# Two regroupings and two weight sums moved later, and the first batch's last score tiles in two bank pairs, in a fused attention and gated feed-forward kernel

## The chip, the core and the metric

The kernel runs on one core of a Trainium2 chip. The metric is device microseconds for one execution. Inputs and output are float32 in DRAM, and the products run in bfloat16.

## The reference

```
q, k, v: (8, 12, 448, 64)         w_gate, w_val: (768, 1536)      w_out: (1536, 768)
scores = (q @ k^T) / sqrt(64)
attn   = relu(scores)^2 / 448
o      = attn @ v                                  # per batch and head
x      = o.transpose(0, 2, 1, 3).reshape(3584, 768)
gate   = relu(x @ w_gate);  val = x @ w_val
out    = (gate * val) @ w_out
```

## The kernel before

There are eight batches of 448 tokens and twelve heads. For each batch the kernel makes attention scores, squares their positive part, multiplies with the values into x (768 features of 448 tokens, features on partitions), makes the gated hidden layer hT (1536 x 448) in twelve units, and for every two batches the output product.

TensorE (PE) works on 64x64 quarters: one call of `mm4` issues four matmuls of 64x448 that run at the same time in the four quarters of the array. The text calls four such matmuls a **pass**. The pieces are:

- A **score tile** (`tile_of`) is one pass: 64 keys of four heads against 448 queries, into a pair of PSUM banks. There are 21 for a batch. `relu2` then lets ScalarE (ACT) take the positive part of the pair into `r_sb` (line 234, four buffers), and VectorE (DVE) squares it into `attn` (line 235).
- **Values** (`value_passes`): seven passes over the seven score tiles of four heads, into one bank pair. In the first batch the pair is always banks 6 and 7, called `both`. The result is copied out of PSUM into x: in the first batch by one instruction (lines 660 and 674), later half by ACT (line 268) and half by DVE (line 269). `exchange` (line 263) then copies each half of the partitions into the other half of a second tile, as two DVE instructions.
- A **unit** (`gv_unit`) is twelve passes that accumulate gate in one bank and val in the other bank of a pair. At its end ACT takes relu of gate (line 327) and DVE multiplies it with val into hT (line 328). Two bank pairs, 6-7 and 4-5, take turns (`acc`), so a unit cannot begin in its pair before line 328 of the unit before the last has read it. Score tiles and values of batches from 1 on take turns in banks 0-1 and 2-3 (`sc_later`).

The order on every engine is written out by hand: `pin` keeps the instructions of an engine in program order. In `spread`, the passes of the units of batch b-1 are walked through one by one, and events of batch b (score tiles, values, regroupings, loads) are put in front of the pass (unit, number) that they are listed with. `last` is the last unit of the walk, and `step` adds passes to such a place.

- **Regrouping** (`regroup`, line 180): k and q of a batch are loaded token by token, and before their transposition DVE copies each into `kr` or `qr`, in two halves of 128x1536. `transpose_grouped` then issues DMA transposes from the SP queue. `turned(b, units, place_of_k, place_of_q)` puts the first half of each at its place and the second five passes later.
- **Weight sums** (`weight_sums`, line 352): four sums over blocks of w_out, 128x2304 each. Numbers 0 and 2 stand among the units of the walk with b == 2, numbers 1 and 3 in the first output product. Number 0 needs the first half of w_out, number 2 needs the second half and the result of number 0. w_out is loaded from the POOL queue after `hold(2)`, an instruction that waits for the DMA transposes of batch 2.

The first batch has no batch before it (`first_batch`). Its score tiles take turns in three bank pairs, 0-1, 2-3 and 4-5 (`sc_first`). `tile(n)` issues a tile, `scored()` its `relu2`. `passes(u, n)` issues the next n passes of unit u. Units 0, 1 and 2 begin here, in banks 4-5, 2-3 and 0-1, with the heads of the first two value groups (`BEGUN`). Four passes of each use x, four use the exchanged x, and four more the third value group.

Of the kernel before, what the change touches and what calls it, by code (L numbers as in the profile page):

```python
# [11 lines left out]
AF = mybir.ActivationFunctionType  # L12
# [4 lines left out]
def kernel(  # L17
# [22 lines left out]
    nc = tc.nc  # L40

    B, H, S, D = q.shape
# [8 lines left out]
    NC = S // 64  # L51
# [14 lines left out]
    HALVES = [(c, slice(c * 64, c * 64 + 64)) for c in range(2)]  # L66

    def pin(ins):
        return tc.keep_in_program_order(ins)
# [60 lines left out]
    def load_nat(dst, src, b, h0, h1):  # L130
        lo = src[b, h0:h1, 0:256, :].rearrange("h (j i) d -> j h i d", i=4)
        hi = src[b, h0:h1, 256:448, :].rearrange("h (j i) d -> j h i d", i=3)
        dma_in(dst[0:64, h0:h1, :, :], lo)
        dma_in(dst[64:128, h0:h1, 0:3, :], hi)

    def natural(b):

        return b if b < NB else 0

    def load_qk(b, h0=0, h1=H):  # L140
        load_nat(kn_b[natural(b)], k, b, h0, h1)
        load_nat(qn_b[natural(b)], q, b, h0, h1)
# [47 lines left out]
    def rotation(numbers):  # L190

        turn = [0]

        def take():
            n = numbers[turn[0] % len(numbers)]
            turn[0] += 1
            return banks[:, n:n + 2, :]
        return take

    sc_first, sc_later, acc = rotation((0, 2, 4)), rotation((0, 2)), rotation((6, 4))  # L200

    def transposes(b, hp, bank):

# [49 lines left out]
    def value_passes(b, qd, ps, i0, i1):  # L253

        attn, v_sb = attn_of(b, qd), v_b[b % NB]
        for i in range(i0, i1):
            mm4([ps[:, r, :S] for r in range(2)], lambda r, c: v_sb[:, 2 * qd + c, i, :],
                lambda r, c: attn[:, 2 * i + c, :], i == 0, i == NC - 1)

    def exchange(b, qd):  # L260
        x0, x1 = (x_of[b][e][qd] for e in range(2))
        for (_, p), (_, other) in zip(HALVES, HALVES[::-1]):
            pin(nc.vector.tensor_copy(x1[p], x0[other]))  # L263

    def values(b, qd, ps):
        value_passes(b, qd, ps, 0, NC)
# [16 lines left out]
    def idle_matmuls(ps, n):  # L283

        for _ in range(n):
            mm2(ps[:, :S], blank[:, 0:128], blank, True, True)


    x_of, hT_of = {}, {}
# [50 lines left out]
    KH = KF // 2  # L340
# [4 lines left out]
              .rearrange("p (f m) -> p f m", m=OH) for c in range(2))  # L345
    B11, B12, B21, B22 = (wo_sb[r][:, :, c * OH:c * OH + OH] for r in range(2) for c in range(2))

    def weight_sums(n):

        o, a, b, op = ((T1, B12, B11, ALU.subtract), (B12, B22, B12, ALU.subtract),  # L350
                       (T2, B22, T1, ALU.subtract), (T4, B21, T2, ALU.subtract))[n]
        pin(nc.vector.tensor_tensor(o, a, b, op))

    def half_sums(o, a, b, op, s, halves=(0, 1)):
        for f in (slice(n * KH // 2, (n + 1) * KH // 2) for n in halves):
# [260 lines left out]
    def first_batch(units):  # L616


        def passes(u, n):
            for _ in range(n):  # L620
                units[u].pop(0)()

        def bank(n):
            return banks[:, n, :]

        def tile(n, at=None):
            todo.append(tile_of(0, n, sc_first() if at is None else banks[:, at:at + 2, :]))

        todo = []

        def scored():
            relu2(*todo.pop(0))

        def second_by_dve():
            src, dst = todo.pop(1)
            r = rpool.tile([128, 2, S], BF16, name="r_sb")
            pin(nc.vector.tensor_scalar(r, src, 0.0, None, ALU.max))  # L637
            scored()
            pin(nc.vector.tensor_tensor(dst, r, r, ALU.mult))

        idle_matmuls(bank(6), 12)
        first_transposes((6, 7, 5, 4))
        idle_matmuls(bank(2), 4)
        tile(0)
        tile(1)
        both = banks[:, 6:8, :]
        for n in range(2, 19):
            tile(n)
            if n in (3, 5, 7, 9):
                hp = n // 2 + 1  # L650
                transposes(0, hp, bank(6 + hp % 2))
            if n in (12, 17):
                value_passes(0, n // 14, both, 0, NC)
            if n == 2:
                second_by_dve()
            elif n > 3:
                scored()
            if n in (12, 17):
                qd = n // 14
                pin(nc.vector.tensor_copy(x_of[0][0][qd], both[:, :, :S]))  # L660
        tile(19)
        scored()
        passes(0, 4)
        scored()
        tile(20, 0)
        scored()
        value_passes(0, 2, both, 0, 4)
        scored()
        passes(1, 4)
        value_passes(0, 2, both, 4, NC)  # L670
        passes(2, 4)
        exchange(0, 0)
        exchange(0, 1)
        pin(nc.scalar.activation(x_of[0][0][2], both[:, :, :S], AF.Copy))
        exchange(0, 2)
        for n in range(4):
            for u in range(2):
                passes(u, 2)
# [13 lines left out]
    def hold(b):  # L692

        for t in range(2):
            pin(nc.gpsimd.tensor_copy(flag[:, t:t + 1], T_b[b % NB][:, t, HP - 1, S - 1:S]))  # L695
# [30 lines left out]
    def turned(b, units, *at):  # L726

        def piece(t, h):
            regroup(b, t, h)
            transpose_grouped(b, t, h)  # L730
        return [(*step(units, u, n, 5 * h), lambda t=t, h=h: piece(t, h)) for t, (u, n) in enumerate(at) for h in range(2)]
# [28 lines left out]
    units = gv_units(0)  # L760
# [5 lines left out]
    for b in range(1, B - 1):  # L766
        if b < B - 3:
            new_x(b)
        units = units[2:] if b == 1 else gv_units(b - 1)
        last = len(units) - 1  # L770
        if b < B - 4:
            first, behind = {1: (24, 105), 2: (40, 132)}.get(b, (0, 132))
            events = paced(units, first, behind, stream(b, b + 1))
            events.append((last, 8 if b == 1 else 5, values_event(b, NQ - 1)))
        else:
            todo = [e for e in attention if e[:2] <= ENDS[b]]
            del attention[:len(todo)]
            if b == B - 4:
                begun = flat(kn_b[1], 4, S)
                x_of[b + 1] = [[begun[:, 2 * e:2 * e + 2, :]] for e in range(2)]  # L780
                del attention[[e[3] for e in attention].index(NC)]
            events = paced(units, 0, 144 if b == B - 3 else 132, todo)
            if b != B - 3:
                events.append((last, 5, values_event(*((b + 1, 0) if b == B - 4 else (B - 1, NQ - 1)))))
        if b == 1:
            events += [(1, 2, lambda: transpose_batch(1))]
            events += turned(2, units, (last - 3, 7), (last - 2, 7))
            events += [(last, 2, lambda: (hold(2), load_v(2), load_wo(), load_qk(3)))]
        elif b == 2:
            events += [(1, 1, lambda: load_v(3))]  # L790
            events += [(last - 5 + 2 * n, 6, lambda n=n: weight_sums(2 * n)) for n in range(2)]
            events += [(last - 1 + t, 3 + 5 * h, lambda t=t, h=h: regroup(3, t, h)) for t in range(2) for h in range(2)]
            events += [(last, 10, lambda: [transpose_grouped(3, t, h) for t in range(2) for h in range(2)])]
        elif b == 3:
            events += [(2, 1, lambda: (hold_unit(2, 1), hold(3), load_qk(4), load_v(4)))]
            events += turned(4, units, (6, 1), (7, 1)) + [(8, 4, lambda: (hold(4), load_qk(5)))]
        elif b == 4:
            events += [(0, 4, lambda: load_v(5))]
            events += turned(5, units, (2, 1), (3, 1)) + [(5, 4, lambda: (hold(5), load_qk(6)))]
            events += turned(6, units, (last - 1, 5), (last, 5))  # L800
        elif b == 5:
            events += [(2, 1, lambda: (hold_unit(4, 1), load_v(6), hold(6), load_qk(7)))]
            events += turned(7, units, (last - 4, 6), (last - 3, 6))
            later = [xpool.tile([128, HP, S], BF16, name=f"x{n}") for n in range(2)]
            x_of[b] = [x_of[b][e] + quads(later[e])[1:] for e in range(2)]
            x_of[B - 2] = [quads(t)[:1] for t in later]
        elif b == 6:
            events += [(3, 1, lambda: (hold(7), load_v(7)))]
            new = [xpool.tile([128, HP, S], BF16, name=f"x{n}") for n in range(2)]
            x_of[b] = [x_of[b][e] + quads(new[e])[1:] for e in range(2)]  # L810
            x_of[B - 1] = [quads(flat(t, HP, S)) for t in (kr, qr)]
        spread(units, events)
        if b == 2:
            out_pair(0, flat(kn_b[1], KH, S), [lambda: weight_sums(1), lambda: weight_sums(3)])
        elif b == 4:
            out_pair(2, flat(v_b[0], KH, S))
# [48 lines left out]
```

## Time and profile before

| | |
|---|---|
| median of 3 runs | 402.62 us (402.38 to 403.21) |
| the profiled execution's own time | 400.59 us |
| its span, first to last instruction | 398.8 us |
| PE busy | 388.0 us (97% of the span) |
| DVE busy | 302.7 us (76%) |
| ACT busy | 243.6 us (61%) |
| POOL busy | 97.4 us (24%) |
| mean granted TensorE clock | 0.997 |

Times in the text are microseconds from the start of the span of the profiled execution. A matmul of 64x448 is shown with about 0.35 us, but passes follow each other at 0.19 us (20 matmuls of x and gv from 92.61 to 93.58, five passes), since matmuls are pipelined. So the idle time that the profile shows before a matmul is shorter than what the wait costs. The cost is the distance between starts less the passes in between at 0.19 us each.

### The profile page before, as it was taken

The page shows a single profiled execution, that of the slowest core. Times are in us where ns is not written, and L with a number is a line of the kernel's source. Part 1 is how long each engine was busy: PE and PEld are TensorE (multiplying, and loading weights), DVE is VectorE, ACT ScalarE, POOL GpSimd, SP SyncE. Part 2 cuts the span into 40 slices and gives each one's busy share as a digit, 9 for nine tenths or more (in the row PEclk, how much of TensorE's full clock was granted, in tenths as well). Part 3 has the DMA queues.
Part 4 walks back from the last instruction along what each step waited for, and adds up shares of the span by engine and source line. Part 5 has one row for each costly group of instructions (what it writes and reads, how often), then busy time and mean ns, then how long its engine had stood idle before and what let it go on. Part 6 is the DMA issues. An engine that isn't in the chain of part 4 may idle for free.

```text
span 398.8 us, 16429 instructions
## 1 busy us (share of the span) xinstructions
PE 388.0 (97%) x7304; PEld 283.7 (71%) x7304; DVE 302.7 (76%) x530; ACT 243.6 (61%) x358; POOL 97.4 (24%) x168
## 2 busy tenths in 40 slices
PE   7799999999999999999999999999999999999995
PEld 3456677787776666679977666988887766777664
DVE  5976886699944686887882578888889869997922
ACT  4963993886334776988632688899873233444231
POOL 8933301700213600503041260020003130000213
PEclk9999999999999999999999999999999999999998
DMA  9999994999836896998962598560002340000035
GB/s 152 181 196 196 198 196 84 154 206 175 152 84 170 106 161 87 147 148 107 133 156 77 150 123 103 117 82 5 2 3 60 79 145 2 3 3 2 21 95 167
DMA packets 90872, 44.17 MB, mean 111 GB/s; under 512 B 55424, under 2 KB 89792, under 8 KB 90800
## 3 DMA queue, kind: packets, MB, share of 16 engines
q0 software_dynamic: 51264, 28.83, 50.4%
q1 hardware_dynamic: 39104, 13.99, 19.4%
q8 instruction: 57, 0.93, 1.0%
q10 hardware_dynamic: 432, 0.30, 0.3%
q14 instruction: 15, 0.12, 0.1%
HBM read 47.19 MB, written 11.01 MB: 146 GB/s over the span
## 4 chain that ended last, share of the span: by engine, by line
PE 87%; DVE 5%; DMA 3%; ACT 2%; issue 1%; POOL 0%; ACTq 0%; DVEq 0%; POOLq 0%
PE ps L72 86%; DMA qn<-in_q_dram 3%; DVE attn L235 2%; ACT r_sb L234 2%; PE ps L208 1%; DVE kqT L209 1%; DVE x L269 0%; ACT g_sb L327 0%; DVE r_sb L637 0%; DVE hT L328 0%; DVE x L660 0%; POOL kn L116 0%; POOL qn L116 0%; PE ps L217 0%; DVE qr L180 0%
## 5 line engine op out<-in xcount | busy, mean ns | idle before, releaser
L72 PE MATMUL ps<-x,gv 64*64 64x448 bf16 (+1 forms) x3336 | 198.1, 349 | 0.7 <-DVE hT L328 0.4
L72 PEld LDWEIGHTS <-gv 64*64 64x64 bf16 (+1 forms) x3960 | 145.1, 107 | 50.4 <-issue 2.8
L234 ACT ACTIVATE r_sb<-ps 128x896 bf16<-128x896 f32 x167 | 149.0, 933 | 17.8 <-PE ps L72 15.1
L235 DVE TENSOR_TENSOR attn<-r_sb 128x896 bf16<-128x896 bf16 x167 | 101.9, 623 | 29.6 <-ACT r_sb L234 21.9
L416 POOL DMA_DIRECT2D out_dram<-attn x63 | 33.1, 531 | 167.3 <-DVE attn L406 132.5
L72 PE MATMUL ps<-kqT 64*64 64x448 bf16 x672 | 69.1, 351 | 3.4 <-ACT r_sb L234 2.6
L72 PEld LDWEIGHTS <-hT 128*64 128x64 bf16 x1056 | 55.9, 110 | 20.9 <-issue 1.4
L402 ACT ACTIVATE attn<-ps 128x384 f32<-128x384 f32 (+1 forms) x64 | 28.8, 450 | 64.5 <-PE ps L72 63.9
L72 PE MATMUL ps<-wo,hT 128*64 128x384 bf16 (+1 forms) x720 | 54.3, 306 | 0.0
L328 DVE TENSOR_TENSOR hT<-ps,g_sb 128x448 bf16<-128x448 f32 x72 | 44.6, 620 | 9.3 <-ACT g_sb L327 8.6
L327 ACT ACTIVATE g_sb<-ps 128x448 bf16<-128x448 f32 x72 | 39.2, 546 | 16.7 <-PE ps L72 16.4
L406 DVE TENSOR_TENSOR attn<-ps,attn 128x384 f32<-128x384 f32 (+1 forms) x48 | 22.8, 505 | 32.5 <-ACT attn L402 17.9
L72 PEld LDWEIGHTS <-vn 64*64 64x64 bf16 (+1 forms) x888 | 35.9, 107 | 11.4 <-issue 1.3
L72 PEld LDWEIGHTS <-kqT 64*64 64x64 bf16 x672 | 28.3, 106 | 14.5 <-issue 5.8
L72 PE MATMUL ps<-attn,vn 64*64 64x448 bf16 x672 | 37.7, 350 | 0.1
L535 ACT ACTIVATE kqT<-ps 128x896 f32<-128x896 f32 x18 | 16.5, 917 | 25.0 <-PE ps L72 25.0
L116 POOL DMA_DIRECT2D vn<-in_v_dram x36 | 23.6, 679 | 17.2 <-PE ps L72 6.6
L72 PE MATMUL ps<-o_ring,hT 128*64 128x384 bf16 (+1 forms) x336 | 26.0, 306 | 0.0
L695 POOL COPY flag<-kqT 128x1 bf16<-128x1 bf16 x12 | 3.3, 288 | 89.5 <-DMA kqT<-kr 50.0
L539 DVE TENSOR_TENSOR kqT<-ps,kqT 128x896 f32<-128x896 f32 x18 | 19.6, 1086 | 5.9 <-PE ps L72 4.2
L116 POOL DMA_DIRECT2D qn<-in_q_dram x20 | 14.8, 762 | 1.3 <-POOLq L849 0.8
L263 DVE COPY x<-x 64x896 bf16<-64x896 bf16 x34 | 13.4, 394 | 1.8
(101 smaller groups left out, 287.3 us busy)
## 6 DMA issues: line engine op xcount, KB each, us to landing
out_dram<-attn POOLq DMA_DIRECT2D x48, 96.0 KB, 2.5
out_dram<-attn SPq DMA_DIRECT2D x48, 96.0 KB, 2.5
kn<-in_k_dram POOLq DMA_DIRECT2D x7, 384.0 KB, 6.6
qn<-in_q_dram POOLq DMA_DIRECT2D x7, 384.0 KB, 9.4
vn<-in_v_dram POOLq DMA_DIRECT2D x14, 192.0 KB, 8.8
gv<-in_moe_w_gate_dram POOLq DMA_DIRECT2D x6, 384.0 KB, 11.8
gv<-in_moe_w_val_dram POOLq DMA_DIRECT2D x6, 384.0 KB, 12.0
wo<-in_moe_w_out_dram POOLq DMA_DIRECT2D x2, 1152.0 KB, 14.1
```

The lines of the kernel that those rows point to most:

```text
L72: pin(nc.tensor.matmul(o, lhsT=l, rhs=r, start=start, stop=stop, skip_group_check=True))
L116: pin(nc.gpsimd.dma_start(out=o, in_=i))
L234: pin(nc.scalar.activation(r, src, AF.Relu))
L235: pin(nc.vector.tensor_tensor(dst, r, r, ALU.mult))
L263: pin(nc.vector.tensor_copy(x1[p], x0[other]))
L327: pin(nc.scalar.activation(g_sb, o[0], AF.Relu, scale=float(out_scale)))
L328: pin(nc.vector.tensor_tensor(hT[:, mf, col:col + S], o[1], g_sb, ALU.mult))
L402: pin(nc.scalar.activation(out_of(t, r, c), bank(P, t), AF.Copy))
L406: pin(nc.vector.tensor_tensor(o, bank(Q, t), o, ALU.add))
L416: pin(engines[c].dma_start(out=rows[:, c0:c1, :], in_=src))
L535: pin(nc.scalar.activation(held(n, j), both(PQ[n][0]), AF.Copy))
L539: pin(nc.vector.tensor_tensor(k, both(PQ[n][1]), k, ALU.add))
```

## The change

Four things change. Values and hidden layer are computed as before, with the same number of matmuls.

1. In the walk with b == 1, the regrouping of q of batch 2 stands five passes later, from (last-2, 7) to (last-1, 0). In the walk with b == 4, k of batch 5 is regrouped two passes later and q three passes later.
2. Weight sums 0 and 2 are each made in two halves of 128x1152. They stood at (last-5, 6) and (last-3, 6). The halves stand at (last-4, 0) and (last-4, 5), and at (last-2, 0) and (last-2, 5).
3. In the first batch, the tiles 17 to 20 go to banks 2-3, 0-1, 2-3 and 0-1 instead of 4-5, 0-1, 2-3 and 0-1. Banks 4-5 are given to unit 0 after tile 14. The second value group is split: four passes, two passes of unit 0, tile 17, three passes. Two more passes of unit 0 stand between tiles 19 and 20. The four passes of unit 2 stand ahead of the last three value passes of the third group instead of behind them.
4. One of the two copies of the first `exchange` goes to ACT.

The rotation of the first tiles begins with banks 2-3 instead of 0-1, and the idle matmuls ahead of them move from bank 2 to bank 0 with it.

```diff
-    sc_first, sc_later, acc = rotation((0, 2, 4)), rotation((0, 2)), rotation((6, 4))
+    sc_first, sc_later, acc = rotation((2, 0, 4)), rotation((0, 2)), rotation((6, 4))
...
-    def exchange(b, qd):
+    def exchange(b, qd, first=None):
         x0, x1 = (x_of[b][e][qd] for e in range(2))
-        for (_, p), (_, other) in zip(HALVES, HALVES[::-1]):
-            pin(nc.vector.tensor_copy(x1[p], x0[other]))
+        for (c, p), (_, other) in zip(HALVES, HALVES[::-1]):
+            if first is not None and c == 0:
+                pin(first.activation(x1[p], x0[other], AF.Copy))
+            else:
+                pin(nc.vector.tensor_copy(x1[p], x0[other]))
...
-    def weight_sums(n):
+    def weight_sums(n, h=None):
...
-        pin(nc.vector.tensor_tensor(o, a, b, op))
+        f = slice(0, KH) if h is None else slice(h * KH // 2, (h + 1) * KH // 2)
+        pin(nc.vector.tensor_tensor(o[:, f], a[:, f], b[:, f], op))
...
-        idle_matmuls(bank(2), 4)
+        idle_matmuls(bank(0), 4)
         tile(0)
         tile(1)
         both = banks[:, 6:8, :]
-        for n in range(2, 19):
+        for n in range(2, 17):
             tile(n)
...
-            if n in (12, 17):
-                value_passes(0, n // 14, both, 0, NC)
+            if n == 12:
+                value_passes(0, 0, both, 0, NC)
             if n == 2:
                 second_by_dve()
             elif n > 3:
                 scored()
-            if n in (12, 17):
-                qd = n // 14
-                pin(nc.vector.tensor_copy(x_of[0][0][qd], both[:, :, :S]))
-        tile(19)
+            if n == 12:
+                pin(nc.vector.tensor_copy(x_of[0][0][0], both[:, :, :S]))
         scored()
-        passes(0, 4)
+        value_passes(0, 1, both, 0, 4)
+        passes(0, 2)
+        tile(17, 2)
+        value_passes(0, 1, both, 4, NC)
+        pin(nc.vector.tensor_copy(x_of[0][0][1], both[:, :, :S]))
+        scored()
+        tile(18, 0)
+        scored()
+        tile(19, 2)
+        passes(0, 2)
         scored()
         tile(20, 0)
         scored()
         value_passes(0, 2, both, 0, 4)
         scored()
         passes(1, 4)
+        passes(2, 4)
         value_passes(0, 2, both, 4, NC)
-        passes(2, 4)
-        exchange(0, 0)
+        exchange(0, 0, nc.scalar)
         exchange(0, 1)
...
         if b == 1:
-            events += turned(2, units, (last - 3, 7), (last - 2, 7))
+            events += turned(2, units, (last - 3, 7), (last - 1, 0))
         elif b == 2:
-            events += [(last - 5 + 2 * n, 6, lambda n=n: weight_sums(2 * n)) for n in range(2)]
+            events += [(last - 4 + 2 * n, 5 * h, lambda n=n, h=h: weight_sums(2 * n, h)) for n in range(2) for h in range(2)]
         elif b == 4:
-            events += turned(5, units, (2, 1), (3, 1)) + [(5, 4, lambda: (hold(5), load_qk(6)))]
+            events += turned(5, units, (2, 3), (3, 4)) + [(5, 4, lambda: (hold(5), load_qk(6)))]
```

## The prediction

> **What bounds the kernel.** I read the page first, then the waits of PE, then DVE's timeline around each wait. From the page, part 1:
>
> ```profile
> PE 388.0 (97%) x7304; PEld 283.7 (71%) x7304; DVE 302.7 (76%) x530; ACT 243.6 (61%) x358; POOL 97.4 (24%) x168
> ```
>
> The waits of PE between 52 and 180 us (who waited for whom, total, times, longest):
>
> ```profile
> PE ps L72 <- DVE x L269: 0.6, 2, 0.4
> PE ps L72 <- DVE hT L328: 0.4, 1, 0.4
> ```
>
> PE is the bound nearly everywhere, so a change pays only by what it takes out of PE's few waits. Outside the first batch three waits stand out, each behind a DVE instruction. DVE's timeline shows why, at batch 2's q:
>
> ```profile
> 57.23 0.62 DVE L235 TENSOR_TENSOR attn<-r_sb 128x896 bf16<-128x896 bf16 x1
> 58.56 0.56 DVE L180 COPY qr<-qn 128x1536 bf16<-128x1536 bf16 x1 [0.71 <-DMA qn<-in_q_dram]
> 59.04 0.62 DVE L235 TENSOR_TENSOR attn<-r_sb 128x896 bf16<-128x896 bf16 x1
> 59.57 0.62 DVE L328 TENSOR_TENSOR hT<-ps,g_sb 128x448 bf16<-128x448 f32 x1
> ```
>
> At weight sum 2:
>
> ```profile
> 89.06 1.36 DVE L352 TENSOR_TENSOR o_ring<-wo,qn 128x2304 bf16<-128x2304 bf16 x1 [0.36 <-DMA wo<-in_moe_w_out_dram]
> 90.33 1.15 DVE L235 TENSOR_TENSOR attn<-r_sb 128x896 bf16<-128x896 bf16 x2
> 91.41 0.62 DVE L328 TENSOR_TENSOR hT<-ps,g_sb 128x448 bf16<-128x448 f32 x1
> 91.94 0.61 DVE L269 CAST x<-ps 128x448 bf16<-128x448 f32 x1
> ```
>
> At batch 5's q:
>
> ```profile
> 169.10 0.62 DVE L328 TENSOR_TENSOR hT<-ps,g_sb 128x448 bf16<-128x448 f32 x1
> 170.75 0.56 DVE L180 COPY qr<-qn 128x1536 bf16<-128x1536 bf16 x1 [1.03 <-issue]
> 171.23 0.62 DVE L235 TENSOR_TENSOR attn<-r_sb 128x896 bf16<-128x896 bf16 x1
> 171.77 0.62 DVE L269 CAST x<-ps 128x448 bf16<-128x448 f32 x1
> ```
>
> Each time DVE stands still for a load (the third is called issue, but the chain of waits has batch 5's q load just ahead of it). Work that was ready queues behind it, and at its end stands the instruction that PE needs. What the first wait costs is read from PE's timeline:
>
> ```profile
> 59.29 0.57 PE L72 MATMUL ps<-x,gv 64*64 64x448 bf16 x6
> 60.24 1.70 PE L72 MATMUL ps<-x,gv 64*64 64x448 bf16 x30 [0.38 <-DVE hT L328]
> 61.60 0.73 PE L72 MATMUL ps<-attn,vn 64*64 64x448 bf16 x10
> ```
>
> The 36 matmuls from 59.29 to 61.60 are 9 passes, 1.71 us at 0.19, and took 2.31: the wait costs 0.60. By the same count the tile and five passes from 91.81 to 93.58 took 1.77 instead of 1.13, a loss of 0.64, and those from 171.86 to 173.41 took 1.55, a loss of 0.42.
>
> The first batch, on PE:
>
> ```profile
> 19.98 0.38 PE L72 MATMUL ps<-kqT 64*64 64x448 bf16 x4 [0.43 <-ACT r_sb L234]
> ...
> 22.41 1.04 PE L72 MATMUL ps<-x,gv 64*64 64x448 bf16 x16 [0.34 <-ACT r_sb L234]
> ```
>
> On ACT:
>
> ```profile
> 17.30 7.49 ACT L234 ACTIVATE r_sb<-ps 128x896 bf16<-128x896 f32 x9
> ```
>
> On DVE:
>
> ```profile
> 21.73 1.09 DVE L660 CAST x<-ps 128x896 bf16<-128x896 f32 x1 [0.29 <-PE ps L72]
> 22.74 2.76 DVE L235 TENSOR_TENSOR attn<-r_sb 128x896 bf16<-128x896 bf16 x5
> ```
>
> ACT takes one tile every 0.81 us without a break until 24.79, and DVE is nearly as full. PE waits for banks. Counted back by 0.81, the relus of tiles 14 to 20 end at 19.93, 20.74, 21.55, 22.36, 23.17, 23.98 and 24.79.
>
> **Batch 2's q (five passes later).** In the changed order the next square (relu ended 57.73) and line 328 (its gate relu ended 58.17) go first. The square starts at 57.77, line 328 at 58.31 and ends at 58.93. PE wants it at about 59.5, so the whole 0.60 goes. The first half of q follows at 58.84 and its load has landed by 58.5. What is next late: the values at 61.0 need the last square by their seventh pass, 62.1. Its relu ends at 60.60 and the square by about 61.5. The move also delays the DMA transposes of q behind the second half, which now ends near 60.4. SP issues its four q transposes from 59.84 to 66.05, one in about 1.5 us, so the third, which needs that half, is due near 63: 2.5 us of cover. So `hold(2)` on POOL and the loads behind it do not move.
>
> **Weight sum 2 in halves.** The queue now is: square, square, line 328, half sum, line 269. The second square waits for its relu (88.96 to 89.87) and starts at 89.91. Squares follow each other at 0.54, so line 328 starts at 90.45 and the half at 90.98. The price of a half has a row: 128x1152 in bf16 on line 356 takes 0.75, less the usual overlap of 0.08. Line 269 starts at 91.65 and ends at 92.27 instead of 92.55. PE still waits, 0.28 less. Bounds: 0.64 if the half slips behind line 269's need, and -0.02 if the price of splitting, 2 x 0.75 - 1.36 = 0.15 for each of the two sums, all lands here. I take 0.28, the worked queue. The load is no limit: PE's 0.8 us gained earlier bring the half to 90.2, 1.2 after its data. The second half goes between two squares at 93.7 and delays the next line 328 from 94.56 to about 94.9, against a need at about 96.5.
>
> [...]
>
> **Batch 5's q (three passes later).** The next square (relu ended 169.70) goes ahead of the q copy, in the time that DVE stood still. Then q at 170.75 as before, since the load binds, and line 269 at 171.23, ending 171.85 instead of 172.38. PE wants it at about 171.8. Gain 0.40 of 0.42. Bounds 0.1 and 0.42, for the DMA chain ahead of that load may shift by some tenths. k two passes later has its own load long landed and costs nothing. SP's q transposes began at 175.67, over 4 us after the copy, and do not notice.
>
> **First batch.** PE's course is worked out as before, in order. Tile 16 at 19.17 as now; four value and two unit passes to 20.50 (banks 4-5 free at 19.93, gv landed 19.95); tile 17 waits for 20.79 (0.29); three value passes to 21.55; tile 18 at 21.60 (0.05); tile 19 waits for 22.41 (0.62). The next two unit passes need the cast of the second value group. It starts at 21.78 behind the values, practically where it starts now, and ends at 22.87, so they wait until 22.92 (0.32). From there PE runs through: tile 20 at 23.30, four value passes, eight unit passes from 24.25 (banks free at 23.98 and 24.79), three value passes to 26.3. The exchanged x is ready by 26.1, since the half on ACT (some 0.95, from a 128x896 row of 0.92) fits behind 24.79. The waits sum to 1.28. Before, from tile 16 on, they are 0.62 (19.36 to 19.98), 0.54 (21.87 to 22.41) and three short ones of 0.33 between 22.6 and 26.7: 1.49. The fillers moved into one gap, and the cast and the two pairs opened others. Gain 0.2. Bounds -0.3 (a slip of tile 20's relu) and +0.45 (the cast's wait gone). The DVE copy that goes to ACT had cover anyway.
>
> **Sum.** 0.2 + 0.60 + 0.28 + 0.40 = 1.48. The profiled execution, 400.59 with a span of 398.8, would become 399.1 and 397.3. The median, 402.62, stands 2.0 above that execution; taken off it, 401.1.
>
> **Rivals.**
>
> *The loads do not come earlier.* If batch 5's q landed at a fixed time, the 1.08 us gained until then would be waited off again: PE would go on at 171.91 instead of 172.44, and 0.53 in all would be left: 402.1. For it: the q copy waits for nothing else. Against: the load was issued after DMA transposes that began at 143.96 behind a DVE copy paced by PE, so the chain moves with PE. Also here: the first-batch gain is absent and both casts stay late, with about the same sum. Chance 0.15.
>
> *Two bank pairs starve ACT (slower).* Place: tiles 17 to 20. A pair's round is 0.05 + 0.38 for the tile + 0.06 + 0.92 for the relu = 1.41 against 2 x 0.81 = 1.62. It decides where PE comes to a refill more than 0.2 late. If each relu then stood alone, ACT would need 1.41 a tile, 4 x 0.60 = 2.4 more, ending at 27.19. Unit 2's passes could start at 27.24, and with 33 passes behind that the batch would end 1.9 later, net of 1.28 gained: 403.3. For it: PE comes to tile 20 0.13 late, behind the cast. Against: the other three refills arrive ahead of their bank. Chance 0.12, of which 0.08 lies over 403.43.
>
> *More goes.* If the first batch's bound and the half sum's both came out high, 400.5. Chance 0.05.
>
> **Numbers.** The forecast has 0.68. A measurement tells apart about 0.2%, 0.8 us. Faster by more than that: 0.68 less 0.03 for its tail, plus 0.05, 0.70. Slower: 0.08. The same: the fixed loads, the rest of the starving and the tail, 0.22. The range goes from 400.5, all upper bounds, to 402.3, the fixed loads with 0.2 of scatter.
>
> **What would show it.** Right: no wait of PE on line 328 near 59; line 269 still waited for near 91, with about 0.3 less; none near 171; ACT's relus without a break until about 24.8, and the transposes of batch 1 at about 31.4 instead of 31.65. Wrong: gaps between ACT's relus after 21, a q copy still held by its load with a PE wait behind it, or a new wait in batch 2 on line 328.

## The result, and the profile after

| | before | after |
|---|---|---|
| median, lowest and highest of 12 runs each, side by side | 401.06 us (400.36 to 403.21) | 399.73 us (398.97 to 400.83) |
| the profiled execution: time, span | 400.59 us, 398.8 us | 399.31 us, 397.5 us |

The ratio is 0.9958, with a 95% interval of 0.9942 to 0.9974: faster by 0.42%. The predicted size, 1.48 us, agrees with the 1.33 between the medians. The predicted time, 401.1 us, does not: 399.73 lies 0.8 under the lower end of the range. The three runs that gave the level of 402.62 are the three highest of the twelve; the other nine lie between 400.36 and 401.91.

The page's first part, after:

```profile
PE 387.9 (98%) x7304; PEld 283.5 (71%) x7304; DVE 302.2 (76%) x531; ACT 244.3 (61%) x359; POOL 97.1 (24%) x168
```

PE does the same work in a span that is 1.3 shorter. The view of PE's waits between 52 and 180 us, which had two rows before, has none. In the changed file lines 263, 268, 269, 327, 328, 352, 660 and 674 are lines 266, 271, 272, 330, 331, 356, 663 or 669, and 685. DVE's timeline at batch 2's q (start, duration, engine, line, operation, tiles, count, and in brackets the idle time before it with what ended it):

```profile
57.57 1.16 DVE L235 TENSOR_TENSOR attn<-r_sb 128x896 bf16<-128x896 bf16 x2
58.65 0.62 DVE L331 TENSOR_TENSOR hT<-ps,g_sb 128x448 bf16<-128x448 f32 x1
59.48 0.56 DVE L180 COPY qr<-qn 128x1536 bf16<-128x1536 bf16 x1 [0.21 <-DMA qn<-in_q_dram]
```

The copy still stands 0.21 for its load, but line 331 has gone ahead of it. PE then runs through, 36 matmuls in one group, where before a group ended at the wait:

```profile
59.63 1.98 PE L72 MATMUL ps<-x,gv 64*64 64x448 bf16 x36
```

DVE at weight sum 2, and at batch 5's q:

```profile
90.00 0.62 DVE L331 TENSOR_TENSOR hT<-ps,g_sb 128x448 bf16<-128x448 f32 x1
90.53 0.75 DVE L356 TENSOR_TENSOR o_ring<-wo,qn 128x1152 bf16<-128x1152 bf16 x1
91.20 0.62 DVE L272 CAST x<-ps 128x448 bf16<-128x448 f32 x1
```

```profile
168.99 0.63 DVE L235 TENSOR_TENSOR attn<-r_sb 128x896 bf16<-128x896 bf16 x1
169.54 0.55 DVE L180 COPY qr<-qn 128x1536 bf16<-128x1536 bf16 x1
170.00 0.62 DVE L272 CAST x<-ps 128x448 bf16<-128x448 f32 x1
```

Neither stands for a load any more. The half sum takes the 0.75 of its row. PE's wait near 91.5 is down to 0.17. Waits are counted here from the start of the last matmul ahead of them to the first behind them, less 0.19 for a pass. The first batch, on PE and on ACT:

```profile
22.66 0.38 PE L72 MATMUL ps<-kqT 64*64 64x448 bf16 x4 [0.43 <-ACT r_sb L234]
23.18 0.57 PE L72 MATMUL ps<-x,gv 64*64 64x448 bf16 x8
...
26.71 5.09 PE L72 MATMUL ps<-x,gv 64*128 64x448 bf16 x52
31.73 0.41 PE L208 MATMUL ps<-ident,kn 128*64 128x128 bf16 x8
```

```profile
14.32 10.71 ACT L234 ACTIVATE r_sb<-ps 128x896 bf16<-128x896 f32 x13
25.06 0.95 ACT L264 ACTIVATE x<-x 64x896 bf16<-64x896 bf16 x1
```

ACT's relus run without a break to 25.03: two bank pairs do not starve it. PE still waits 0.61 ahead of tile 19 (22.66) and 0.32 behind the cast (23.18), both as predicted to 0.01. Batch 1's transposes begin at 31.73, not at the 31.4 expected. This execution was already 0.25 later at tile 16 (19.42 against 19.17), so that from tile 16 on it gained 0.16.

**Stretches instead of times.** The traces differ by up to 0.9 us before tile 16, and one by 2.7, and that hides everything else. So the fourteen traces of this study are compared by stretches, from one start of PE work to another. A stretch that the change does not touch agrees in all of them: from the first output product (100.10 in before) to the values at 168.83 it takes 68.73. The stretches that it does touch, named by their starts in the trace of before; a trace whose own edit changes a stretch in another way is left out of that column:

| old place or form | tile 16 (19.17) to transposes (31.65) | values 53.43 to 61.60 | values 88.98 to 97.18 | values 168.83 to 178.17 |
|---|---|---|---|---|
| before | 12.48 | 8.17 | 8.20 | 9.34 |
| other traces with the old one | 12.48 to 12.57 | 8.09, 8.10, 8.25, 8.32, 11.34 | 8.15, 8.10, 8.27, 7.75 | 8.89 in four |
| traces with the new one | 12.31 to 12.32 in eight | 7.56 in six | 7.80 in six | 8.89 in nine |

### The profile page after: what moved, and what is told of

Its sections match the earlier page's. It is cut to its first block, busy times and chain, and to the rows that moved or that the text cites. A ratio compares the mean times of both kernels' runs of the same rounds, so it can differ in the third digit from the quotient of the medians.

```text
span 397.5 us, 16431 instructions
## 1 busy us (share of the span) xinstructions
PE 387.9 (98%) x7304; PEld 283.5 (71%) x7304; DVE 302.2 (76%) x531; ACT 244.3 (61%) x359; POOL 97.1 (24%) x168
## 4 chain that ended last, share of the span: by engine, by line
PE 94%; ACT 2%; DVE 1%; DMA 1%; issue 1%; POOL 0%; POOLq 0%
PE ps L72 92%; ACT r_sb L234 2%; DMA qn<-in_q_dram 1%; PE ps L208 1%; DVE attn L235 0%; DVE x L669 0%; DVE r_sb L641 0%; DVE kqT L209 0%; PE ps L217 0%; ACT g_sb L330 0%; DVE attn L643 0%; POOL qn L116 0%; DVE attn L410 0%; POOLq L860 0%
## 5 line engine op out<-in xcount | busy, mean ns | idle before, releaser
L72 PEld LDWEIGHTS <-gv 64*64 64x64 bf16 (+1 forms) x3960 | 143.1, 107 | 48.8 <-issue 1.6
L72 PE MATMUL ps<-kqT 64*64 64x448 bf16 x672 | 65.7, 351 | 2.8 <-ACT r_sb L234 2.6
L72 PEld LDWEIGHTS <-vn 64*64 64x64 bf16 (+1 forms) x888 | 34.7, 107 | 11.7 <-issue 1.3
L72 PEld LDWEIGHTS <-kqT 64*64 64x64 bf16 x672 | 25.7, 107 | 14.2 <-issue 5.0
```

The lines of the kernel that those rows point to most:

```text
L72: pin(nc.tensor.matmul(o, lhsT=l, rhs=r, start=start, stop=stop, skip_group_check=True))
```

## The experiments

All ran on chips of the same kind, each with runs of the kernel before beside them (medians 401.17, 401.40 and 401.03 for the three groups). An interval is of the ratio to those.

**The level: both kernels again, unchanged.**

> The kernel before, unchanged, against itself. Theory (the level shown before the change, 402.62, was drawn from the upper part of a spread of about 399.5 to 403): ratio 1.000 within 0.002, median near 401.1, and a trace in which the wait near 59.5 (0.5 to 0.6) is there again, the one near 172 (0.42) perhaps not, since it was absent from three traces with batch 5's q in its old place. Rival (402.6 is the level and 401.1 a chance): median at 402 or more.

Measured: 400.72 us (399.89 to 403.94), ratio 0.999 (0.997 to 1.0009); the profiled execution 400.41. The wait near 59.5 is there (0.47), the one near 172 is not.

> The changed kernel, unchanged, on the same chip and beside the same runs as the single parts. Theory (the whole gains what was measured first, 0.4%): ratio 0.994 to 0.998, median near 399.7. Rival (the parts measured alone, -0.44, -0.40, 0 and +0.28 us, add up to 0.6 us and nothing more is there): ratio near 0.9985.

Measured: 399.47 us (398.70 to 400.37, 7 runs), ratio 0.996 (0.9944 to 0.9976); the profiled execution 398.70 with a span of 396.9. What follows: the gain repeats. In four groups the kernel before had a median of 401.03 to 401.40, and 402.62 was a draw of three from the upper end of its spread.

**One part at a time on the kernel before.** The first batch as in the change, nothing else:

```diff
+    sc_first, sc_later, acc = rotation((2, 0, 4)), rotation((0, 2)), rotation((6, 4))
...
+        tile(17, 2)
...
+        tile(18, 0)
...
+        exchange(0, 0, nc.scalar)
```

> The kernel before with the first batch's new order alone (and the half exchange on ACT). Theory of the forecast: PE's waits between tile 16 and the transposes of batch 1 shrink by 0.2 us and the whole time by as much. Rival, after the trace of the changed kernel: the first batch does come to its end 0.2 us earlier, but the first transposes of batch 1's q then wait for q's load, which DMA brings at its own pace, so that the values of batch 1 begin within 0.1 us of where they would have begun, and the time is the same (between -0.1 and +0.1 us).

Measured: 400.54 us, ratio 0.9989 (0.9968 to 1.001). The time does not resolve it. The trace does: 12.32 from tile 16 to the transposes, against 12.48 to 12.57 in the five traces without it, so 0.16 to 0.25.

The rival has a part in it. The transposes of batch 1 also wait for that batch's q from DMA. From their start to the values at 45 the traces without such a wait take 13.82 or 13.83; this one takes 13.89, the changed kernel's first 14.08, and with the old order two of five take 14.04 and 14.73. From tile 16 to those values the middle of the five traces with the old order is 26.36, and of seven with the new one 26.21. So some 0.15 of the gain is left behind that load, and in a single execution it can be waited off.

```diff
-            events += turned(2, units, (last - 3, 7), (last - 2, 7))
+            events += turned(2, units, (last - 3, 7), (last - 1, 0))
```

> The kernel before with batch 2's q regrouped five passes later, nothing else. Theory: line 328 no longer stands behind the q copy, PE's loss near 59.5 us goes whole, the time falls by 0.6 us, and the weight sum's wait near 91 stays at 0.64 or grows (PE comes earlier, the second half of w_out does not). Rival: the wait moves to the next instruction behind the q copy and less than 0.3 us is won.

Batch 2's q alone. Measured: 400.26 us, ratio 0.999 (0.9971 to 1.0009), inconclusive by itself; the stretch from the values at 53.43 takes 7.56, 0.5 to 0.8 less than in the traces with the old place, and PE's wait is gone.

```diff
...
-            events += [(last - 5 + 2 * n, 6, lambda n=n: weight_sums(2 * n)) for n in range(2)]
+            events += [(last - 4 + 2 * n, 5 * h, lambda n=n, h=h: weight_sums(2 * n, h)) for n in range(2) for h in range(2)]
```

> The kernel before with weight sums 0 and 2 in halves at their later places, nothing else. Theory of the forecast: the cast of line 269 still stands behind one half sum, PE's loss near 91.8 us falls from 0.64 to about 0.35, gain 0.3 us (0.4 by the trace of the changed kernel). [...]

The sums alone, with the two halves of `weight_sums` as in the change. Measured: 400.60 us, ratio 1.0 (0.9974 to 1.0026). The stretch from the values at 88.98 takes 7.80. The profiled execution took 404.77, with a span of 403.0: batch 2's q, here in its old place, landed at 61.93, and PE waited 2.44 for the line 328 behind it:

```profile
63.73 3.19 PE L72 MATMUL ps<-x,gv 64*64 64x448 bf16 x30 [2.29 <-DVE hT L328]
```

The windows of that stage show what came on top. Each line has a window and its length, the busy time of PE, PEld, DVE, ACT and POOL, the granted clock of PE (the share of its full speed that it was given), and the share and GB/s of DMA:

```profile
61.10:63.70 2.60, 0.34 (x8) 0.00 (x0) 1.65 (x4) 1.52 (x3) 0.00 (x0) 1.00 1.21 186
63.70:65.50 1.80, 1.77 (x20) 1.10 (x23) 1.80 (x4) 0.00 (x0) 0.00 (x0) 0.51 1.29 109
65.50:66.80 1.30, 1.30 (x20) 0.81 (x16) 0.79 (x2) 0.00 (x0) 0.19 (x1) 0.50 0.71 157
```

Behind the wait PE had half its clock for 3.41 us, from 63.75 to 67.16. Passes came 0.37 apart instead of 0.19.

```diff
-            events += turned(5, units, (2, 1), (3, 1)) + [(5, 4, lambda: (hold(5), load_qk(6)))]
+            events += turned(5, units, (2, 3), (3, 4)) + [(5, 4, lambda: (hold(5), load_qk(6)))]
```

> The kernel before with batch 5's regrouping two and three passes later, nothing else. Theory: PE's wait near 172 goes, 0.42 us by the count of passes, and 0.15 more at the next output product, where the two row halves of the array, left out of step by a wait inside a pass, must meet again: 0.55 us in all. Rival without that second piece: 0.4 us. Rival of fixed loads: the copy still waits for its load at the same time, 0.1 us or less.

Batch 5's k and q alone. Measured: 400.95 us, ratio 1.0007 (0.9982 to 1.0031): no gain. The wait near 172 that the term was read from is in the shown profile of before alone. Four other traces with the old place have none. Where it can occur is in this trace's DVE:

```profile
169.75 0.62 DVE L235 TENSOR_TENSOR attn<-r_sb 128x896 bf16<-128x896 bf16 x1
170.67 0.56 DVE L180 COPY qr<-qn 128x1536 bf16<-128x1536 bf16 x1 [0.29 <-DMA qn<-in_q_dram]
```

The load was as late as in before (it landed at 170.59, before at 170.68), and with the new place nobody behind the copy was late. In two traces of the changed kernel's variants with loads as late, the sums whole and batch 2's q earlier still, the cover was just too short: the stretch stayed at 8.89, but the next output product began 0.08 and 0.09 late.

**Batch 2's q, put back and earlier still, on the changed kernel.**

```diff
-            events += turned(2, units, (last - 3, 7), (last - 1, 0))
+            events += turned(2, units, (last - 3, 7), (last - 2, 7))
```

> The changed kernel with batch 2's q alone put back, at (last-2, 7). Theory (one edit carries most of the gain, and the late end of the spread too): the stretch between the values at 53 and at 61 takes 8.1 to 8.3 again instead of 7.57, the median is 0.6 to 0.9 over the changed kernel, about 400.3, and a few runs of a dozen pass 402, which none of 31 runs with the change and the new place did. Rival (the late runs come from elsewhere): 0.5 more in all runs alike, none over 402.

Measured: 400.76 us (399.88 to 402.87), ratio 0.9991 (0.997 to 1.0013), 1.0 to 1.3 over the two medians of the changed kernel; one run of twelve over 402. The stretch takes 8.32. DVE and PE:

```profile
58.73 0.56 DVE L180 COPY qr<-qn 128x1536 bf16<-128x1536 bf16 x1 [0.87 <-DMA qn<-in_q_dram]
...
59.74 0.62 DVE L331 TENSOR_TENSOR hT<-ps,g_sb 128x448 bf16<-128x448 f32 x1
```

```profile
60.41 1.70 PE L72 MATMUL ps<-x,gv 64*64 64x448 bf16 x30 [0.54 <-DVE hT L331]
```

This is the wait of before, put back by one line.

```diff
-            events += turned(2, units, (last - 3, 7), (last - 1, 0))
+            events += turned(2, units, (last - 3, 7), (last - 2, 2))
```

> The changed kernel with batch 2's q regrouped ten passes earlier, at (last-2, 2), five before its old place. Theory (the copy stands on DVE until its load lands, and the place alone sets the wait): the 0.54 of PE's wait near 59.5 in the old place grows by five passes, 0.95, to about 1.5 us; 1.5 us over the changed kernel, about 401.2, ratio 0.9995 to 1.001. Rival (the load moves with DVE's order, or DVE's queue and not the load makes the wait): a wait of at most 0.6, ratio near 0.9975.

Measured: 404.92 us (404.34 to 407.50, 6 runs), ratio 1.0109 (1.0082 to 1.0135). The direction is the theory's, the size is not: five passes earlier than the old place cost over 4 us more than q put back did, not 0.95.

```profile
56.42 0.38 PE L72 MATMUL ps<-kqT 64*64 64x448 bf16 x2
60.49 0.38 PE L72 MATMUL ps<-kqT 64*64 64x448 bf16 x2 [3.69 <-DVE x L272]
```

```profile
58.81 0.56 DVE L180 COPY qr<-qn 128x1536 bf16<-128x1536 bf16 x1 [3.43 <-DMA qn<-in_q_dram]
59.29 0.62 DVE L235 TENSOR_TENSOR attn<-r_sb 128x896 bf16<-128x896 bf16 x1
59.82 0.62 DVE L272 CAST x<-ps 128x448 bf16<-128x448 f32 x1
```

Another waiter stands behind the copy here: not line 331, which PE needs near 59.5, but the cast of the values (line 272), which it needs at 56.45. The price of this copy, which stood 3.43 for its load, was set by the earliest need in the queue behind it, and that goes by instructions, not by passes. The stretch took 13.16, 5.6 more than 7.56. 3.85 is the wait. Again PE had half its clock behind it, from 60.88 to 64.30 (0.50 in the windows 61 to 62, 62 to 63 and 63 to 64), half of these 3.41 us lost, 1.7.

**What the halving of the sums does.** On the changed kernel:

```diff
-            events += [(last - 4 + 2 * n, 5 * h, lambda n=n, h=h: weight_sums(2 * n, h)) for n in range(2) for h in range(2)]
+            events += [(last - 4 + 2 * n, 0, lambda n=n: weight_sums(2 * n)) for n in range(2)]
```

> The changed kernel with the two weight sums whole, each at the place of its first half, (last-4, 0) and (last-2, 0). Theory (the halving pays, since the whole sum takes 1.36 where the half takes 0.75): the cast ahead of PE's wait near 91.5 starts 0.6 later, the wait grows from 0.17 to about 0.75, 0.6 us over the changed kernel. Rival (the later place behind the load pays, and the halving nothing): the wait stays under 0.3, the time within 0.2 us of the changed kernel.

Measured: 400.44 us, ratio 0.9974 (0.9956 to 0.9993), 0.7 to 1.0 over the changed kernel. The stretch takes 8.40 and the wait 0.77, as the theory had it:

```profile
90.96 1.35 DVE L356 TENSOR_TENSOR o_ring<-wo,qn 128x2304 bf16<-128x2304 bf16 x1
92.23 0.62 DVE L272 CAST x<-ps 128x448 bf16<-128x448 f32 x1
```

The later place alone gains nothing: it takes the wait for the load away and puts the sum itself in its room. The halving pays.

```diff
-            events += [(last - 4 + 2 * n, 5 * h, lambda n=n, h=h: weight_sums(2 * n, h)) for n in range(2) for h in range(2)]
+            events += [(last - 4 + 2 * n, 5 * h + 3 * n, lambda n=n, h=h: weight_sums(2 * n, h)) for n in range(2) for h in range(2)]
```

> The changed kernel with both halves of weight sum 2 three passes later, so that the first half stands behind the cast of x that PE waits for near 91, and not ahead of it. Theory (the half sum ahead of the cast is all that is left of that wait): the cast starts 0.66 earlier, the wait of 0.17 is gone, the stretch between the values at 88 and at 96 takes 7.63 instead of 7.80; the time 0.2 us less, below what the rounds resolve. Rival (DVE is full and the wait moves on): a new wait on line 331 within the next two units, the stretch 7.8 or more.

Measured: 399.82 us, ratio 0.9969 (0.9949 to 0.9989). The cast starts earlier, the wait of 0.17 is gone and the stretch takes 7.57. But behind it:

```profile
97.33 0.38 PE L72 MATMUL ps<-attn,vn 64*64 64x448 bf16 x4 [0.16 <-DVE attn L235]
```

The next values now wait 0.32 for the last square, and the stretch to the output product takes 3.12 instead of 2.92. 0.03 of the 0.23 is left. The wait moved on, as the rival had it, though not to line 331 but to a square, and the stretch did fall to 7.57: between the two places DVE has no room to spare.

**Waits ahead of the values.** To the edit above:

```diff
...
-        gaps = [{(1, 1): 1, (1, NC): 0.35, (NC, 1): 0.75}[a[3], b[3]] for a, b in zip(events, events[1:])]
+        gaps = [{(1, 1): 1, (1, NC): before_v, (NC, 1): 1.1 - before_v}[a[3], b[3]] for a, b in zip(events, events[1:])]
...
```

(`before_v` is 0.55 for batches 1 and 2, 0.35 for the rest.)

> As the one before, and the values of batches 1 and 2 stand a little later among the passes (share of the gap ahead of them 0.55 instead of 0.35, behind them 0.55 instead of 0.75). Theory (PE's waits ahead of the values near 45, 53 and 80, 0.26, 0.12 and 0.14, are there because the relu two tiles back is still running): they go, 0.5 us, with the sums 0.7 in all, about 398.8, ratio 0.993 to 0.996. Rival (what is taken ahead of the values is lost behind them, where the next tile waits for the casts of x): no gain, ratio 0.9955 to 0.997.

Measured: 399.41 us (398.86 to 399.84), ratio 0.9958 (0.994 to 0.9976): not to be told from the change. The waits went as expected (0.26 to 0.07, 0.12 and 0.14 to none), but 0.46 came back at 62, where the values wait for squares:

```profile
61.01 1.64 PE L72 MATMUL ps<-attn,vn 64*64 64x448 bf16 x24
62.80 0.38 PE L72 MATMUL ps<-attn,vn 64*64 64x448 bf16 x4 [0.15 <-DVE attn L235]
```

In this execution batch 2's q had landed at 60.00, late, and the squares stood behind its copy. Whether the new places or the late load cost the 0.46 is open. If it was the load, the cover of the moved copy ends ahead of this landing, 6.46 behind the values.

**The first exchange.** On the changed kernel:

```diff
-        exchange(0, 0, nc.scalar)
+        exchange(0, 0)
```

> The changed kernel with both halves of the first exchange on DVE as before. Theory (that copy had cover, as the prediction said; the gain of the first batch comes from the order of PE's passes): the distance from tile 16 to batch 1's transposes stays at 12.31 to 12.35, against 12.48 to 12.57 before. Rival (the half on ACT made the gain): the second exchange ends 0.4 later, and the distance goes back to 12.5.

Measured: 399.45 us, ratio 0.9963 (0.9944 to 0.9983). The distance is 12.46, nearly that of before. The passes behind the exchange:

```profile
28.11 1.74 DVE L266 COPY x<-x 64x896 bf16<-64x896 bf16 x4
```

```profile
28.99 5.23 PE L72 MATMUL ps<-x,gv 64*128 64x448 bf16 x52
```

The same 52 matmuls take 5.23 instead of 5.09. So in this one trace 0.14 of the first batch's 0.2 comes from the half exchange on ACT, and the order of PE's passes brought the rest, 0.02 to 0.11. (All times of this trace are some 2 us late, since PE had half its clock from 7.28 to 10.69, ahead of the stretch; its mean over the execution is 0.995.)

## Why the prediction was right, and where it was wrong

**The step that failed** is the last of the sum: "The median, 402.62, stands 2.0 above that execution; taken off it, 401.1." The steps before it gave the profiled execution as 399.1 with a span of 397.3. Measured are 399.31 with 397.5, and 398.70 with 396.9. The distance of 2.0 was put on both kernels as if it were a fixed offset. It was mostly a draw: over the four groups the median of before stands 0.4 to 0.8 above 400.59. Taken from 401.06, the level measured beside the change, the same 1.48 gives 399.58, and 399.73 was measured. The range did not cover this, because it varied the terms and gave the level none of its own, though the three runs (402.38 to 403.21) and the profiled execution already stood 1.8 and more apart. Nor is the distance a property of both kernels alike. The old places turn the landing of a load into PE time, one for one, so a late landing makes a late run, and the change takes that away. For batch 2's q, with the landing counted from the start of the values at 53:

| old place | landing behind the values | stretch | difference |
|---|---|---|---|
| before | 5.01 | 8.17 | 3.16 |
| before, again | 4.93 | 8.09 | 3.16 |
| first batch alone | 4.94 | 8.10 | 3.16 |
| batch 5's q alone | 5.09 | 8.25 | 3.16 |
| q put back | 5.16 | 8.32 | 3.16 |
| sums alone | 6.91 | 11.34 | 4.43 (1.3 of it at half clock) |

In the new place landings of 4.95 to 5.58 all give 7.56. One late run has its trace: the profiled execution of the sums alone, 404.77, was the latest of its twelve, and the late landing cost it 3.2 over the stretch of before and 0.4 more at half clock behind it. The twelve runs of the changed kernel beside those of before spread over 1.9 us, those of before over 2.9. Of 165 runs with the old place 32 passed 402 us, of 79 with the new one 1; the runs with q earlier still and one run of before at 2319 us, far outside all others, are not counted. Some of that is the lower level, and the three high runs of before left no trace, so that they lost their 2 us at this wait is likely and not shown.

**The size, 1.48.** It agrees with the 1.33 partly by luck: the 0.40 of batch 5's q is not there in most executions, and the terms of batch 2's q and of the sum were too small.

**Batch 2's q, 0.60.** Right in mechanism, and somewhat small: 0.53 to 0.76 in the four ordinary traces at the old place other than before's 0.61, and 0.07 more between the values at 61 and those at 80 (18.86 against 18.79), which q put back shows to belong to this edit. DMA transposes and `hold(2)` kept their cover in most traces; in the changed kernel's first one the chain was 1.4 later against PE (the copy of `hold(2)` at 69.62 instead of 68.56, PE 0.3 ahead).

**Weight sum 2, 0.28.** The queue was right (sum, then the cast, at 0.66), the size was not: 0.30 to 0.47 in four pairs, -0.05 in one. "The load is no limit" was wrong for the old place. There too the stretch is the landing of w_out's second half plus 8.21: landings 0.11 ahead of the values at 88.98 to 0.06 behind them gave 8.10 to 8.27, and one 0.54 ahead gave 7.75. In the changed kernel it landed 1.62 and 0.48 behind them, which the new place took without loss. The price of the split, 2 x 0.75 against 1.35 for the whole, is there, but off the path: with the sums whole the stretch is 0.6 longer. Here the rival of loads at fixed times was half right: in both traces of the changed kernel this load lost ground against PE.

**Batch 5's q, 0.40.** It holds for one execution. If this wait too goes one for one with the landing, it opens where q lands more than 1.40 behind the values at 168.83 (1.85 - 0.45). In fourteen traces q landed that late four times (1.74 to 1.88), and between -0.41 and 0.78 ten times. In the four the load was also issued late, 7.0 to 7.6 ahead of those values, against 7.4 to 8.8 in the ten; what held the issue back is open. So the edit is worth an estimated 0.5 to 0.6 (0.45 and the 0.15 of the last section, less 0.08 where the cover is too short) in three executions of ten, and nothing in the others. A wait seen in one profile was taken for a property of the kernel.

**First batch, 0.2.** Right in size up to the transposes (some 0.15 is left by the values at 45), and mostly wrong in cause: "The DVE copy that goes to ACT had cover anyway" is refuted, since that copy brought 0.14. The waits of PE that were worked out one by one were met to 0.01 (0.62 and 0.32, measured 0.61 and 0.32; tile 17's 0.29 was 0.12 to 0.26).

**Slower rival.** Starving needed gaps between ACT's relus, and there are none.

By the middle of the traces the terms are 0.2 for the first batch, 0.6 and 0.07 for batch 2's q, 0.35 for the sum and 0 for batch 5's q: some 1.2. The two differences of medians are 1.33 and 1.93. That late landings in the runs of before make up the rest is likely and not shown.

## What to carry to other kernels

A copy that stands for its load holds up what its engine has behind it (by 3.43 us on DVE with q earlier still) and should be put behind every instruction that another engine needs soon; ask for the earliest need behind it, and how late the load can be, not how late it was once. Before a wait seen in one profile is priced, look whether the load behind it lands with scatter: such a wait is a share of executions, not a constant. And a change that removes waits for loads can remove spread too (1.9 us over twelve runs here, 2.9 before), so a median of few runs is no offset to add to it; take the level from many runs, and prove small parts by stretches between fixed points of the trace, which agree to 0.01 us where times scatter by 1.

## What was not expected of the hardware

- Half clock behind a single wait: PE ran at a granted clock of 0.50 for 3.41 us after idle times of 2.3 us (sums alone) and of 3.7 (q earlier still). A wait of 2.44 thus cost 4.2: 3.78 in its stretch (11.34 against 7.56) and 0.41 in the next, to the values at 80 (19.27 against 18.86).
- Shorter idle times left the clock at 1.00: in the trace of before the longest between two matmuls are 0.66 (ahead of 5.62) and 0.64 (ahead of 9.20), and the clock from 0 to 396 is 1.00. What the clock goes by is not shown.
- Passes out of step behind a wait. Where the wait at 172 ends inside a pass in the trace of before, four matmuls are shown with 0.54 instead of 0.36 from there on. Each still takes 0.35 and the pace is unchanged, but the four of the first row below start within 0.01 of each other (170.721 to 170.731), those of the second within 0.19 (173.415 to 173.600):

```profile
170.72 0.36 PE L72 MATMUL ps<-kqT 64*64 64x448 bf16 x4
...
173.41 0.54 PE L72 MATMUL ps<-kqT 64*64 64x448 bf16 x4
```

  The next output product then begins late: 19.73 behind those values instead of 19.58 for the same passes, 0.15 on top of the wait's 0.45. In the two traces with a shorter delay there (0.43 instead of 0.36) it begins at 19.66 and 19.68. In the traces of before and of the changed kernel the product's first matmul, of 128 rows, begins 0.28 behind the last start of the 64-row matmuls ahead of it (197.62 to 197.90, and 196.29 to 196.57). The last four of those start within 0.16 of each other in before and within 0.01 in the other, which is the 0.15.
